# Eight heads as eight 64 x 32 tiles of the TensorE array, in place of block-diagonal pairs

## The chip, the cores and the metric

One core of a Trainium2 chip runs the kernel. The metric is the device time of one execution in microseconds; lower is better. Every time here is of a run on the chip or of its trace.

## What is computed

Eight batches of 576 tokens, eight heads of 64. Each head has 32 packing queries `p` of its own. All products are in fp32, and the answer has the shape [4608, 512].

```python
p_packed = sm_attn(p, k, v)                # 32 packed values for each head, from 576 tokens
out = sm_attn(q, p_packed, p_packed)       # every token attends to the 32 packed values of its head
x = out as [B * S, H * D]                  # 4608 tokens of 512
logits = x @ w_gate; e_idx = argmax(logits)            # 8 experts, one for each token
for e in range(E):
    h = relu(x[mask] @ w1[e])              # 512 -> 1024
    out[mask] = gate_w * eom * (h @ w2[e]) # 1024 -> 512
```

## The kernel before

The work of a batch has three parts, written as Python generators that yield an estimate of their time, and traced in turn so that one batch's attention lies between the matmuls of another's experts. While `ffn(b)` is traced, `route(b + 1)` and `encode(b + 2)` are advanced along with it, up to three quarters of the way (`r1`, `e1`), and at its end `values_up(b + 1)` is merged in. The first batches have their order written out by hand (`CFG["order"]`), with matmuls on zeros (`keep_warm`) where TensorE would wait. Within the traced order a scheduler may put a ready instruction ahead of one that is not.

- `encode(b)` (L254) makes the packed values. The eight heads are two groups g of four, and a group is two pairs c of heads. `p` is copied into `pb`, which holds for each pair 128 rows (two heads of 64 dimensions) and 64 columns (two heads of 32 queries), zero off the diagonal blocks (L257 to L260). `scores` (L234) multiplies it with `k`: one 128-row, 64-column product for a pair, the two pairs beside each other in the columns of the array (`beside`, L79), for half of the tokens (288) at a time, into one PSUM bank. `soft` (L263) is the softmax of a group: the maximum on DVE (L267), the exponential on ACT with its sum (L273). `turn` (L281) transposes it on TensorE, `pack` (L297) multiplies with `v` (`ps_pp`), and L302 scales and masks the result to the two heads' own blocks (`mask`). `expand_T` (L242) transposes both groups; `ppT` is then block-diagonal in the same way as `pb`. `ps_pg` (L329) is the router's product, and `guess` (L337) chooses the expert whose weights the batch loads first: that of evenly weighted packed values.
- `route(b)` (L350): `match` (L363) multiplies `ppT` with `q` (`ps_s2T`), again for each pair; DVE transposes it in blocks of 32, and `soft` (L371) is the softmax over the 32 packed values. `ps_lg` (L401) is the router.
- `values_up(b)` (L504) multiplies `ppT` with the first weights of the guessed expert (`ps_G`), since the attention's weights can be applied after them; `split` (L65) makes of it a high and a low part (`Gh` by ACT, `Gl` by DVE), for products that need one pass. `ffn(b)` (L521) is then `ps_h` (attention's weights with `G`), relu on ACT and DVE, and `ps_o` (second weights).
- Tokens whose expert is not the batch's go through `leftover` (L595) at the end.

PSUM has eight banks, in two tags: `a` with `NA = CFG["pa"] = 3` banks, for the attention, and `f` with the other five, for `ps_h`, `ps_o`, `ps_G` and the scores of the first batches. Loads are issued on SP's queue in the order of the trace; `fetch` (L190) issues one tile of `k`, `q` or `v` where one is given up.

The lines that put products beside each other:

```python
def beside(dsts, seqs):
    for j, row in enumerate(zip(*seqs)):
        for dst, (a, m) in zip(dsts, row):
            res = nc.tensor.matmul(dst, a, m, start=j == 0, stop=j == len(seqs[0]) - 1)
def sides(ps):
    return [ps[c * M2:(c + 1) * M2] for c in range(GP)]      # M2 = 64, GP = 2
```

Of the kernel before, what the change touches and what calls it, by code (L numbers as in the profile page):

```python
# [9 lines left out]
F32 = mybir.dt.float32  # L10
# [10 lines left out]
CFG = dict(pre='kkkkqqkkkk', last=(4, 2, 3), warm=(8, 2, 2, 2, 2, 2), raw=8, a1T=2, rq=2, pa=3, wst=3, w1=6,  # L21
# [10 lines left out]
def tile_packed_attn_then_moe(ctx, tc, qT, kT, v, v_rem, pT, w_go, w1, w2, out):  # L32
    """qT, kT: [B, NG, (2 D), HG / 2, S]; v: [B, NG, 128, TF, (HG D)], its last tokens in v_rem;
    pT: [B, (2 D), H / 2, NP]; w_go: [128, DM / 128, 2 E]; w1, w2: [E, chunk, 128, 2, 512]."""
    nc = tc.nc
    B, NG, _, GP, S = qT.shape
    NPAIR, NP = pT.shape[2:]
# [27 lines left out]
    def split(hi, lo, src, hi_eng=None, lo_eng=None):  # L65
        """src = hi + lo, each of the width that a single-pass product takes."""
        (hi_eng or nc.scalar.copy)(hi, src)  # L67
        (lo_eng or nc.vector).tensor_tensor(lo, src, f(hi), ALU.subtract)  # L68
# [10 lines left out]
    def beside(dsts, seqs):  # L79
        """Products that stand beside each other in the array's columns, in turn."""  # L80
        for j, row in enumerate(zip(*seqs)):
            for dst, (a, m) in zip(dsts, row):
                res = nc.tensor.matmul(dst, a, m, start=j == 0, stop=j == len(seqs[0]) - 1)  # L83
        return res

    def sides(ps):
        return [ps[c * M2:(c + 1) * M2] for c in range(GP)]
# [14 lines left out]
    def keep_warm(b, i):  # L102
        """Work for the tensor engine while the first batch has it wait, for its clock's sake."""
# [13 lines left out]
    odd = const.tile([P, HG], F32, name="odd")  # L117
    nc.gpsimd.memset(odd, 1.0)
    nc.gpsimd.affine_select(out=odd, in_=odd, pattern=[[-NP, HG]], compare_op=ALU.is_ge,
                            fill=0.0, base=0, channel_multiplier=1)  # L120
    nc.gpsimd.affine_select(out=odd, in_=odd, pattern=[[NP, HG]], compare_op=ALU.is_ge,
                            fill=0.0, base=NP - 1, channel_multiplier=-1)
    mask = const.tile([P, 2, 1], F32, name="mask")
    for i in range(2):
        nc.gpsimd.tensor_tensor(mask[:, i], odd[:, i:i + 1], odd[:, i + 2:i + 3], ALU.add)
# [7 lines left out]
    pb = const.tile([P, NPAIR, 2, NP], F32, name="pb")  # L133
    nc.gpsimd.memset(pb, 0.0)
# [34 lines left out]
    pp_d = tc.dram_tile([B, P, NG, P], F32, name="pp_d")  # L169
# [3 lines left out]
    def beyond(gen):  # L173
        """A step of gen, queued behind the anchors."""
# [15 lines left out]
    def fetch(x):  # L190
        """The next of the loads of k, v and p or of q, in the order of their use."""
# [6 lines left out]
        if x == "v":  # L198
            t = sb.tile([P, T, HG * D], F32, tag=tag, name="vt", bufs=bufs)
            nc.sync.dma_start(t[:, 0:TF], v[b, g])  # L200
            nc.sync.dma_start(t[:REM, TF], v_rem[b, g])
        else:
            t = sb.tile([P, GP, S], F32, tag=tag, name=x, bufs=bufs)
            src = (kT if x == "k" else qT)[b, g]
            step = 1 if b == 0 else GP
            for c in range(0, GP, step):
# [35 lines left out]
    def expand_T(b, src, nm):  # L242
        """[(h n), (2h d)] of the groups, zeros but for a row's own head -> [(2h d), group, (h n)]."""
        ps = bank(f"ps_{nm}")
        pv = ps[:, :NG * P].rearrange("p (g n) -> p g n", n=P)
        for g in range(NG):
            t = nc.tensor.transpose(pv[:, g], src[g], ident)  # L247
        anchor(b, t)
        keep_warm(b, 4)
        x = sb.tile([P, NG, P], F32, tag="ppT", name=nm, bufs=CFG["tt"])  # L250
        anchor(b, nc.scalar.copy(x, pv))
        return x

    def encode(b):  # L254
        """p, k, v of a batch -> packed values, transposed and block-diagonal."""
        pt = take("p", b, 0) if ("p", b, 0) in loaded else (fetch("k"), take("p", b, 0))[1]
        for i in range(2):  # L257
            rows = slice(i * D, (i + 1) * D)
            eng(b, "p").tensor_copy(pb[rows, :, i], pt[rows])
        pbs = [pb.rearrange("p c i n -> p c (i n)")[:, c] for c in range(NPAIR)]  # L260
        ppbd = []

        def soft(g, kTs):  # L263
            s1 = [scores(b, pbs[g * GP:(g + 1) * GP], kTs, "s1", "a" if b > 1 else "f", hf) for hf in range(2)]
            nm2 = sb.tile([P, 2], F32, tag="nm2", name="nm2", bufs=2)
            for hf in range(2):
                nc.vector.tensor_reduce(nm2[:, hf:hf + 1], s1[hf], axis=AX.X, op=ALU.max, negate=True)  # L267
            nmx = sb.tile([P, 1], F32, tag="nmx", name="nmx", bufs=2)
            anchor(b, nc.vector.tensor_scalar(nmx, nm2[:, 0:1], nm2[:, 1:2], QK, ALU.min, ALU.mult))
            a1 = sb.tile([P, 2, HS], F32, tag="row", name="a1", bufs=CFG["row"])  # L270
            sm = sb.tile([P, 2], F32, tag="sm", name="sm", bufs=2)
            for hf in range(2):
                anchor(b, nc.scalar.activation(a1[:, hf], s1[hf], AF.Exp, bias=nmx, scale=QK, accum_out=sm[:, hf:hf + 1]))  # L273
            if g == NG - 1:
                keep_warm(b, 1)
            rs = sb.tile([P, 1], F32, tag="rs", name="rs", bufs=2)
            nc.vector.tensor_scalar(rs, sm[:, 0:1], sm[:, 1:2], 1e-9, ALU.add, ALU.add)
            nc.vector.reciprocal(rs, rs)
            return a1, rs

        def turn(g, a1):  # L281
            """The softmax of a group, transposed."""
            a1f = a1.rearrange("p a b -> p (a b)")
            ps = bank("ps_a1T")
            pv = ps.rearrange("p (t n) -> p t n", n=P)
            pr = bank("ps_a1T")
            for t_ in range(TF):
                nc.tensor.transpose(pv[:, t_, :], a1f[:, t_ * P:(t_ + 1) * P], ident)  # L288
            anchor(b, nc.tensor.transpose(pr[:REM, :P], a1f[:, SF:S], ident))
            at = sb.tile([P, T, P], F32, tag="a1T", name="a1T", bufs=CFG["a1T"])  # L290
            copy = nc.vector.tensor_copy if b == 0 else nc.scalar.copy
            anchor(b, copy(at[:, 0:TF], pv))
            anchor(b, copy(at[:REM, TF], pr[:REM, :P]))
# [3 lines left out]
        def pack(g, at, rs, vt):  # L297
            pp = bank("ps_pp")[:, :P]
            anchor(b, beside(sides(pp), [[(at[:n, t_, c * M2:(c + 1) * M2], vt[:n, t_, c * P:(c + 1) * P])
                                          for t_ in range(T) for n in (P if t_ < TF else REM,)] for c in range(GP)]))  # L300
            bd = sb.tile([P, 2, D], F32, tag="bd", name="ppbd", bufs=CFG["bd"])
            anchor(b, nc.vector.scalar_tensor_tensor(bd, pp.rearrange("p (h d) -> p h d", d=D), rs,  # L302
                                                     mask.to_broadcast([P, 2, D]), op0=ALU.mult, op1=ALU.mult))
            bd = bd.rearrange("p h d -> p (h d)")
            ppbd.append(bd)
            nc.sync.dma_start(pp_d[b, :, g], bd)

        xs = []
        for g in range(NG):
            ks = pairs("k", b, g)  # L310
            yield Y["k"]
            xs.append(soft(g, ks))
            yield Y["s1"]
        ats = []
        for g in range(NG):
            ats.append(turn(g, xs[g][0]))
            yield Y["a1T%d" % g]
        for g in range(NG):
            vt = take("v", b, g)
            follow("v", b)  # L320
            pack(g, ats[g], xs[g][1], vt)
            yield Y["pp"]
        x = expand_T(b, ppbd, "ppT")
        ppT = [x[:, c // GP, c % GP * M2:(c % GP + 1) * M2] for c in range(NPAIR)]
        yield Y["ppT"]
        ps_g = bank("ps_pg")
        pg_v = ps_g[:, :NG * 2 * E].rearrange("p (g e) -> p g e", e=2 * E)
        for g in range(NG):
# [538 lines left out]
```

## Time and profile before

| | us |
|---|---|
| median of 3 runs | 481.17 (479.87 to 481.31) |
| span of the profiled execution, first to last instruction | 478.5 |
| TensorE busy (PE), matmuls | 465.0, 97% |
| weight loads (PEld) | 342.0, 71% |
| VectorE (DVE) | 286.5, 60% |
| ScalarE (ACT) | 166.4, 35% |
| GpSimd (POOL) | 101.2, 21% |
| DMA queue of the loads, share of 16 engines | 48.9% |

The profiled execution's own time is its span; 2.67 us lie between it and the median of the runs. PE is TensorE's matmuls, PEld its weight loads, which overlap them. A row of a group gives the line, engine, operation, output<-inputs, the tile of the array that an instruction uses (rows*columns), the shape of what it reads, and behind the bar the busy time in us and the mean ns of one; busy time counts overlapping instructions once. A row of the timeline gives start and length in us and, behind x, how many of the kind it merges. Clock 1.00 is the full TensorE clock.

### The profile page before, as it was taken

The numbers are of one execution on the slowest core, as the hardware profiler recorded it, in microseconds if no ns is written. First come the engines' busy times: TensorE is split into PE (matmuls) and PEld (weight loads), VectorE is DVE, ScalarE is ACT, GpSimd is POOL, SyncE is SP. The second block draws the span as 40 slices with busy tenths as digits, with TensorE's granted clock in tenths as the row PEclk, the third lists the DMA queues.
The fourth block names the chain that finished last, engine by engine and source line by source line (L and its number), as shares of the span: only waits on it lengthen the run. The fifth ranks groups of instructions, "written<-read, shape, count | busy, mean of one in ns | idle before, by whom it ended". The sixth has DMA issues, their size and how long they took to land.

```text
span 478.5 us, 8004 instructions
## 1 busy us (share of the span) xinstructions
PE 465.0 (97%) x2864; PEld 342.0 (71%) x2864; DVE 286.5 (60%) x793; ACT 166.4 (35%) x376; POOL 101.2 (21%) x99
## 2 busy tenths in 40 slices
PE   6999999999999999999999999999999999979996
PEld 4648766878667785878767786777858885765755
DVE  4594784697367645575457644586457846971221
ACT  2174343524224333243225333353333333410310
POOL 6114110621007200341006200160004400410000
PEclk8999999999999999999999999999999999979999
DMA  8899992549506950197404920186102920255101
GB/s 260 287 391 379 372 340 64 176 170 381 171 28 216 400 171 6 53 358 271 134 12 154 367 82 3 33 293 241 50 12 79 344 74 11 68 186 205 41 5 53
DMA packets 39113, 83.05 MB, mean 174 GB/s; under 512 B 3999, under 2 KB 18719, under 8 KB 39072
## 3 DMA queue, kind: packets, MB, share of 16 engines
q1 hardware_dynamic: 39040, 82.52, 48.9%
q8 instruction: 23, 0.38, 0.3%
q14 instruction: 18, 0.15, 0.1%
q0 software_dynamic: 32, 0.00, 0.0%
HBM read 66.78 MB, written 15.79 MB: 173 GB/s over the span
## 4 chain that ended last, share of the span: by engine, by line
PE 92%; DVE 4%; POOL 2%; ACT 1%; issue 1%; POOLq 0%
PE ps_o L573 36%; PE ps_h L76 22%; PE ps_o L585 7%; PE ps_G L83 6%; PE ps_pp L83 5%; PE ps_s2T L83 4%; PE ps_s L83 4%; PE ps_a1T L288 1%; PE ps_lg L83 1%; PE ps_lo L682 1%; PE ps_lh L682 1%; POOL keys L145 1%; ACT a L273 1%; PE ps_pg L83 1%; PE ps_ppT L247 1%
## 5 line engine op out<-in xcount | busy, mean ns | idle before, releaser
L573 PE MATMUL ps_o<-w2h,hT 128*128 128x512 f32 (+1 forms) x528 | 168.7, 393 | 0.0
L573 PEld LDWEIGHTS ps_o<-w2h,hT 128*128 128x128 f32 x528 | 97.5, 189 | 29.2 <-issue 5.1
L573 PE MATMUL ps_o<-w2l,hT 128*128 128x512 f32 (+1 forms) x264 | 103.0, 390 | 0.0
L542 DVE SCALAR_TENSOR_TENSOR hT<-ps_h,hT 128x256 fp32r<-128x256 f32 x192 | 60.9, 350 | 42.9 <-ACT hT L539 42.1
L68 POOL TENSOR_TENSOR w2l<-wst,w2h 128x1024 fp32r<-128x1024 f32 x25 | 66.2, 2651 | 93.5 <-ACT w2h L67 77.8
L76 PE MATMUL ps_h<-ah,Gh 128*128 128x256 f32 (+1 forms) x256 | 80.6, 315 | 3.4 <-DVE l_dec L630 1.9
L539 ACT ACTIVATE hT<-ps_h 128x320 fp32r<-128x320 f32 (+1 forms) x128 | 51.3, 411 | 92.8 <-PE ps_h L76 91.9
L76 PE MATMUL ps_h<-al,Gh 128*128 128x256 f32 (+1 forms) x256 | 77.7, 303 | 0.0
L76 PE MATMUL ps_h<-ah,Gl 128*128 128x256 f32 (+1 forms) x256 | 76.6, 299 | 0.0
L76 PEld LDWEIGHTS ps_h<-ah,Gh 128*128 128x128 f32 x256 | 48.9, 191 | 17.6 <-issue 7.6
L573 PEld LDWEIGHTS ps_o<-w2l,hT 128*128 128x128 f32 x264 | 50.0, 189 | 9.5 <-issue 0.4
L76 PEld LDWEIGHTS ps_h<-al,Gh 128*128 128x128 f32 x256 | 49.0, 192 | 4.0 <-issue 3.3
L76 PEld LDWEIGHTS ps_h<-ah,Gl 128*128 128x128 f32 x256 | 49.0, 191 | 0.1
L67 ACT CAST w2h<-wst 128x1024 fp32r<-128x1024 f32 x32 | 33.6, 1049 | 44.1 <-PE ps_o L573 37.4
L576 DVE TENSOR_SCALAR ob<-ps_o,scm_all 128x512 f32<-128x512 f32 (+1 forms) x33 | 24.0, 727 | 27.7 <-PE ps_o L573 26.7
L68 DVE TENSOR_TENSOR Gl<-ps_G,Gh 128x512 fp32r<-128x512 f32 x32 | 21.9, 684 | 24.5 <-ACT Gh L67 24.4
L83 PE MATMUL ps_G<-w,ppT 128*64 128x512 f32 x128 | 33.2, 613 | 0.0
L67 ACT CAST Gh<-ps_G 128x512 fp32r<-128x512 f32 x32 | 18.8, 587 | 28.3 <-PE ps_G L83 28.2
L432 POOL TENSOR_TENSOR g_d<-L,g_mx 128x40 f32<-128x40 f32 x8 | 2.1, 266 | 124.0 <-DVE g_mx L418 124.0
L384 POOL TENSOR_TENSOR s<-s,sm 128x576 f32<-128x576 f32 x14 | 16.2, 1159 | 52.5 <-DVE sm L383 46.8
L585 PE MATMUL ps_o<-w2h,hT 128*128 128x512 f32 x64 | 27.2, 425 | 0.0
L585 PE MATMUL ps_o<-w2l,hT 128*64 128x512 f32 x64 | 24.1, 394 | 0.0
(170 smaller groups left out, 527.4 us busy)
## 6 DMA issues: line engine op xcount, KB each, us to landing
w<-in_w_dram SPq DMA_DIRECT2D x40, 512.0 KB, 5.7
wst<-in_w_dram SPq DMA_DIRECT2D x32, 512.0 KB, 8.2
vt<-in_v_dram SPq DMA_DIRECT2D x16, 512.0 KB, 5.7
k<-in_kT_dram SPq DMA_DIRECT2D x14, 576.0 KB, 8.3
q<-in_qT_dram SPq DMA_DIRECT2D x14, 576.0 KB, 6.9
out_dram<-ob SPq DMA_DIRECT2D x31, 256.0 KB, 2.2
a_d<-a2T SPq DMA_DIRECT2D x16, 320.0 KB, 4.5
out_dram<-ob SPq DMA_DIRECT2D x10, 128.0 KB, 2.3
```

The source lines that it names most:

```text
L67: (hi_eng or nc.scalar.copy)(hi, src)
L68: (lo_eng or nc.vector).tensor_tensor(lo, src, f(hi), ALU.subtract)
L76: res = nc.tensor.matmul(dst, a, m, start=j == 0, stop=j == len(seq) - 1)
L83: res = nc.tensor.matmul(dst, a, m, start=j == 0, stop=j == len(seqs[0]) - 1)
L145: nc.gpsimd.tensor_scalar(keys.rearrange("p b n -> p (b n)"), key_i, big_id, None, ALU.add)
L384: eng(b, "mul").tensor_tensor(sv, sv, sm.to_broadcast([P, n, NP]), ALU.mult)
L539: nc.scalar.activation(hT[:, :n], ps, AF.Relu)
L542: nc.vector.scalar_tensor_tensor(hT[:, d0:d0 + s1 - s0], ps[:, s0:s1], 0.0, f(hT[:, s0:s1]), op0=ALU.max, op1=ALU.subtract)
L573: nc.tensor.matmul(ps[:, cs], a, m[:, cs], start=i == 0, stop=i == len(seq) - 1)
L576: nc.vector.tensor_scalar_mul(ob[:, cs], ps[:, cs], sc)
L585: nc.tensor.matmul(ps[:n], a, m, start=i == 0, stop=i == len(seq) - 1)
L682: nc.tensor.matmul(ps[i % nq * m:(i % nq + 1) * m], stat[:, i], wt[:, k], start=i < nq, stop=i >= n - nq)
```

## The change

The block-diagonal form goes. A head is now a tile of 64 rows (its dimensions) and 32 columns (its packed values). A group is now the four even or the four odd heads: rows 0 to 63 of a tile hold an even head, rows 64 to 127 the odd one of its pair. `by_head` issues the eight heads' products in turn, a group to a PSUM bank, in column 32c for pair c. `k` and `q` are loaded by halves of the tokens, for all heads, in place of by groups; `encode` scores both halves for both groups before the first softmax. `pack` has products of 32 columns by 64 in place of 64 by 128, both groups in one bank, and no mask. `ppT` is one 128 x 128 transpose in place of two. The last 64 tokens' transposes of both groups share a bank and a copy. `pa` is 4 in place of 3, so tag `f` has four banks. `values_up` takes two banks at a time and yields once for both. `leftover` follows the new layout, with four banks for `xT` in place of two. The host's layout of `q`, `k`, `v`, `w1` follows.

```diff
-CFG = dict(... pa=3, ...)
+CFG = dict(... pa=4, ...)
...
     def sides(ps):
-        return [ps[c * M2:(c + 1) * M2] for c in range(GP)]
+        return [ps[c * NP:(c + 1) * NP] for c in range(NPAIR)]
+
+    def by_head(banks, stat, mov):
+        at = [(g, c) for c in range(NPAIR) for g in range(NG)]
+        return beside([sides(banks[g])[c] for g, c in at],
+                      [[(stat[g * D:(g + 1) * D, c * NP:(c + 1) * NP], mov[c][g * D:(g + 1) * D])] for g, c in at])
...
-    pb = const.tile([P, NPAIR, 2, NP], F32, name="pb")
-    nc.gpsimd.memset(pb, 0.0)
...
-    def scores(b, stat, mov, nm, tag, hf):
-        ps = bank(f"ps_{nm}", tag)[:, :HS]
-        x = beside(sides(ps), [[(stat[c], mov[c][:, hf * HS:(hf + 1) * HS])] for c in range(GP)])
+    def scores(b, stat, mov, nm, tag):
+        ps = [bank(f"ps_{nm}", tag)[:, :HS] for _ in range(NG)]
+        x = by_head(ps, stat, mov)
...
         def turn(g, a1, pr):
...
-            anchor(b, nc.tensor.transpose(pr[:REM, :P], a1f[:, SF:S], ident))
+            anchor(b, nc.tensor.transpose(pr[:REM, g], a1[:, SF:S], ident))
...
+        def pack(pp, g, at, ar, vt):
+            return beside(sides(pp[:, g]), [[(at[:, t_, c * NP:(c + 1) * NP], vt[:, t_, c * D:(c + 1) * D])
+                                             for t_ in range(TF)]
+                                            + [(ar[:REM, g, c * NP:(c + 1) * NP], vt[:REM, TF, c * D:(c + 1) * D])]
+                                            for c in range(NPAIR)])
...
+        s1 = []
+        for hf in range(2):
+            ks = pairs("k", b, hf)
+            yield Y["k"]
+            s1.append(scores(b, pt, ks, "s1", "a" if b > 1 else "f"))
+            for g in range(NG):
+                anchor(b, nc.vector.tensor_reduce(nm2[:, g, hf:hf + 1], s1[hf][g], axis=AX.X, op=ALU.max, negate=True))
+            yield Y["s1"]
+        a1s = [soft(g, s1) for g in range(NG)]
...
+        pr = bank("ps_a1r")[:, :NG * P].rearrange("p (g n) -> p g n", n=P)
         for g in range(NG):
-            ats.append(turn(g, xs[g][0]))
+            ats.append(turn(g, a1s[g], pr))
             yield Y["a1T%d" % g]
+        ar = sb.tile([P, NG, P], F32, tag="a1r", name="a1r", bufs=1)
+        anchor(b, (nc.vector.tensor_copy if b == 0 else nc.scalar.copy)(ar[:REM], pr[:REM]))
+        pp = bank("ps_pp")[:, :NG * D].rearrange("p (g d) -> p g d", d=D)
...
+        anchor(b, nc.vector.tensor_tensor(ppc, pp, rs.to_broadcast([P, NG, D]), ALU.mult))
+        nc.sync.dma_start(pp_d[b], ppc)
...
+        anchor(b, nc.tensor.transpose(ps, ppc, ident))
...
+        ps_g = [bank("ps_pg")[:, :2 * E] for _ in range(NG)]
+        anchor(b, by_head(ps_g, ppT, [wgo[:, c] for c in range(NPAIR)]))
...
         for part in ([0], [1]) if b == 0 else ([0, 1],):
+            for hf in part:
+                match(hf)
+                yield Y["s2T"]
             for g in range(NG):
-                match(g, part)
-                yield Y["s2T"]
                 soft(g, part)
...
         for n in range(DF // BANK):
-            for g in range(NG):
-                ps = bank("ps_G", "f")
-                beside(sides(ps), [[(ppT[g * GP + cc], w1s[(n * NG + g) * GP + cc])] for cc in range(GP)])
+            banks = [bank("ps_G", "f") for _ in range(NG)]
+            by_head(banks, ppT, w1s[n * NPAIR:(n + 1) * NPAIR])
+            for ps in banks:
...
-                yield 0.86
+            yield 0.86
...
-        for cc in range(GP):
-            rows, cs = slice(cc * M2, (cc + 1) * M2), slice(cc, NPAIR, GP)
-            pv = bank("ps_l", "f")[:, :NG * m].rearrange("p (c n) -> p c n", n=m)
-            for g in range(NG):
-                nc.tensor.matmul(pv[:, g], pp[rows, g], at_[rows, g], start=True, stop=True)
-            nc.scalar.copy(xT[:, cs], pv)
+        pv = [bank("ps_l", "f")[:, :m] for _ in range(NPAIR)]
+        for g in range(NG):
+            hd = slice(g * D, (g + 1) * D)
+            beside([x[hd] for x in pv], [[(pp[c * NP:(c + 1) * NP, hd], at_[c * NP:(c + 1) * NP, g])] for c in range(NPAIR)])
+        for c in range(NPAIR):
+            nc.scalar.copy(xT[:, c], pv[c])
```

More of the change, by code (lines that the diff above doesn't have):

```diff
@@ L116, in tile_packed_attn_then_moe @@
     nc.scalar.activation(first, blank[:, 0:1], AF.Exp)
[L117 to L125, printed above, removed]
     ones = const.tile([P, P], F32R, name="ones")
@@ L198, in fetch @@
         if x == "v":
-            t = sb.tile([P, T, HG * D], F32, tag=tag, name="vt", bufs=bufs)
+            t = sb.tile([P, T, NPAIR * D], F32, tag=tag, name="vt", bufs=bufs)
             nc.sync.dma_start(t[:, 0:TF], v[b, g])
@@ L202, in fetch @@
         else:
-            t = sb.tile([P, GP, S], F32, tag=tag, name=x, bufs=bufs)
+            t = sb.tile([P, NPAIR, HS], F32, tag=tag, name=x, bufs=bufs)
             src = (kT if x == "k" else qT)[b, g]
-            step = 1 if b == 0 else GP
-            for c in range(0, GP, step):
+            step = NPAIR // 2 if b == 0 else NPAIR
+            for c in range(0, NPAIR, step):
                 nc.sync.dma_start(t[:, c:c + step], src[:, c:c + step])
@@ L240, in scores @@
         return ps
-    def expand_T(b, src, nm):
-        ps = bank(f"ps_{nm}")
-        pv = ps[:, :NG * P].rearrange("p (g n) -> p g n", n=P)
-        for g in range(NG):
[L247 to L252, printed above, removed]
     def encode(b):
         pt = take("p", b, 0) if ("p", b, 0) in loaded else (fetch("k"), take("p", b, 0))[1]
[L257 to L265, printed above, removed]
-            for hf in range(2):
[L267 to L273, printed above, removed]
@@ L274, in soft, with turn @@
             if g == NG - 1:
                 keep_warm(b, 1)
[L276 to L283, printed above, removed]
+            return a1.rearrange("p a b -> p (a b)")
+        def turn(g, a1, pr):
             ps = bank("ps_a1T")
             pv = ps.rearrange("p (t n) -> p t n", n=P)
-            pr = bank("ps_a1T")
@@ L287, in turn @@
             for t_ in range(TF):
-                nc.tensor.transpose(pv[:, t_, :], a1f[:, t_ * P:(t_ + 1) * P], ident)
-            anchor(b, nc.tensor.transpose(pr[:REM, :P], a1f[:, SF:S], ident))
-            at = sb.tile([P, T, P], F32, tag="a1T", name="a1T", bufs=CFG["a1T"])
+                nc.tensor.transpose(pv[:, t_, :], a1[:, t_ * P:(t_ + 1) * P], ident)
+            anchor(b, nc.tensor.transpose(pr[:REM, g], a1[:, SF:S], ident))
+            at = sb.tile([P, TF, P], F32, tag="a1T", name="a1T", bufs=CFG["a1T"])
@@ L291, in turn @@
             copy = nc.vector.tensor_copy if b == 0 else nc.scalar.copy
-            anchor(b, copy(at[:, 0:TF], pv))
-            anchor(b, copy(at[:REM, TF], pr[:REM, :P]))
+            anchor(b, copy(at, pv))
             keep_warm(b, 2 + g)
             return at
[L297 to L306, printed above, removed]
@@ L320, in encode @@
             follow("v", b)
[L321 to L324, printed above, removed]
+            anchor(b, pack(pp, g, ats[g], ar, vt))
+            if g == 0:
+                yield Y["pp"]
+        ppc = sb.tile([P, NG, D], F32, tag="ppc", name="ppc", bufs=CFG["bd"])
+        anchor(b, nc.vector.tensor_tensor(ppc, pp, rs.to_broadcast([P, NG, D]), ALU.mult))
+        ppc = ppc.rearrange("p g d -> p (g d)")
+        nc.sync.dma_start(pp_d[b], ppc)
+        yield Y["pp"]
+        ps = bank("ps_ppT")[:, :P]
+        anchor(b, nc.tensor.transpose(ps, ppc, ident))
+        keep_warm(b, 4)
+        ppT = sb.tile([P, P], F32, tag="ppT", name="ppT", bufs=CFG["tt"])
+        anchor(b, nc.scalar.copy(ppT, ps))
         yield Y["ppT"]
-        ps_g = bank("ps_pg")
-        pg_v = ps_g[:, :NG * 2 * E].rearrange("p (g e) -> p g e", e=2 * E)
-        for g in range(NG):
-            anchor(b, beside(sides(pg_v[:, g]), [[(ppT[c], wgo[:, c])] for c in range(g * GP, (g + 1) * GP)]))
+        ps_g = [bank("ps_pg")[:, :2 * E] for _ in range(NG)]
+        anchor(b, by_head(ps_g, ppT, [wgo[:, c] for c in range(NPAIR)]))
         keep_warm(b, 5)
         pg = sb.tile([P, NG, 2, 2 * E], F32, tag="pg", name="pg", bufs=CFG["pg"])
-        anchor(b, nc.vector.tensor_copy(pg, pg_v.rearrange("p g (i e) -> p g i e", i=1).to_broadcast([P, NG, 2, 2 * E])))
+        for g in range(NG):
+            anchor(b, nc.vector.tensor_copy(pg[:, g], ps_g[g].rearrange("p (i e) -> p i e", i=1).to_broadcast([P, 2, 2 * E])))
         R[b], packed[b] = (ppT, pg), ppT
@@ L352, in route @@
         qTs = []
-        for g in range(NG):
-            qTs.append(pairs("q", b, g))
+        for hf in range(2):
+            qTs.append(pairs("q", b, hf))
             yield Y["q"]
@@ L359, in route, with match @@
         A[b] = (ah, al)
-        rows = {}
-        def match(g, part):
-            if g not in rows:
-                rows[g] = sb.tile([P, 2, HS], F32, tag="row", name="s2", bufs=CFG["row"])
-            for hf in part:
-                ps = scores(b, ppT[g * GP:(g + 1) * GP], qTs[g], "s2T", "a" if b else "f", hf)
-                nc.vector.transpose(rows[g][:, hf], ps)
+        rows = [sb.tile([P, 2, HS], F32, tag="row", name="s2", bufs=CFG["row"]) for _ in range(NG)]
+        def match(hf):
+            ps = scores(b, ppT, qTs[hf], "s2T", "a" if b else "f")
+            for g in range(NG):
+                nc.vector.transpose(rows[g][:, hf], ps[g])
         def soft(g, part):
```

58 lines of the change are left out of this document (31 added, 27 removed).

## The prediction

> **What bounds the kernel now.** I read the busy shares and the chain first, then the waits of TensorE, then stretches, then the products that the change touches.
>
> ```profile
> span 478.5 us, 8004 instructions
> PE 465.0 (97%) x2864; PEld 342.0 (71%) x2864; DVE 286.5 (60%) x793; ACT 166.4 (35%) x376; POOL 101.2 (21%) x99
> PE 92%; DVE 4%; POOL 2%; ACT 1%; issue 1%; POOLq 0%
> ```
>
> The waits of TensorE (what waited, for what; us in total, times, longest):
>
> ```profile
> PE ps_s L83 <- POOL keys L145: 2.9, 1, 2.9
> PE ps_h L76 <- DVE l_dec L630: 1.9, 1, 1.9
> PE ps_a1T L288 <- ACT a L273: 1.2, 1, 1.2
> ...
> PE ps_h L76 <- DVE ob L576: 1.1, 1, 1.1
> PE ps_h L76 <- DVE hT L542: 0.4, 1, 0.4
> ```
>
> TensorE works or drains in 97% of the span, the chain runs on it for 92%, and each place where it waits for another engine occurs once. So a microsecond taken off TensorE is a microsecond off the end, if nothing else becomes late. By stretches (length, then busy time and count of PE, PEld, DVE, ACT, POOL, then granted clock, DMA share, GB/s):
>
> ```profile
> 5.00:10.00 5.00, 2.21 (x12) 1.49 (x14) 3.10 (x3) 0.00 (x0) 3.62 (x7) 0.82 1.00 347
> 10.00:15.00 5.00, 4.87 (x33) 3.29 (x32) 3.65 (x14) 2.15 (x8) 0.00 (x0) 0.83 1.05 374
> 20.00:25.00 5.00, 3.81 (x32) 2.09 (x31) 4.48 (x17) 1.56 (x5) 1.53 (x3) 1.00 0.50 168
> ...
> 203.10:258.20 55.10, 55.10 (x346) 40.84 (x345) 32.56 (x93) 20.55 (x46) 11.53 (x10) 1.00 0.50 178
> ...
> 368.40:404.00 35.60, 35.60 (x210) 26.36 (x210) 24.08 (x66) 13.18 (x30) 7.28 (x6) 1.00 0.43 156
> 404.00:430.00 26.00, 22.64 (x109) 19.37 (x108) 22.85 (x42) 7.54 (x13) 7.99 (x3) 0.87 0.34 112
> ```
>
> Three regimes: a start in which the DMA engines are full (share near 1) but for about half of 20 to 25 us; a repeating batch of 55.1 us in which PE is busy all the time, DVE at 59% and DMA at 50%; and a tail from 404 us in which DVE (22.85 of 26) plans the leftovers, which the change does not touch. The change is worth what it saves PE up to 404 us.
>
> **How the products run now.** Rows of one batch (start, length, count):
>
> ```profile
> 203.04 1.19 PE L83 MATMUL ps_s2T<-q,ppT 128*64 128x288 f32 x8
> 205.79 0.71 PE L83 MATMUL ps_s<-k,pb 128*64 128x288 f32 x4
> 227.65 2.85 PE L83 MATMUL ps_pp<-vt,a1T 128*64 128x128 f32 x40
> 233.12 0.64 PE L83 MATMUL ps_lg<-a2T,pg 128*32 128x128 f32 x16
> 238.13 1.08 PE L83 MATMUL ps_G<-w,ppT 128*64 128x512 f32 x4
> 239.14 0.44 PE L247 MATMUL ps_ppT<-ident,ppbd 128*128 128x128 f32 x2
> 241.00 1.94 PE L83 MATMUL ps_G<-w,ppT 128*64 128x512 f32 x8
> 250.71 0.41 PE L83 MATMUL ps_pg<-wgo,ppT 128*64 128x16 f32 x8
> 120.28 1.09 PE L83 MATMUL ps_pp<-vt,a1T 128*64 128x128 f32 x16
> ```
>
> The code issues 8 products a batch for ps_G and the trace has 16 matmuls: a product is two matmuls. I call a round one matmul in every tile that runs beside the others. Two tiles are beside each other now, so x8 is four rounds and x4 two: a score round costs (1.19 − 0.71)/2 = 0.24 us and a call's fixed part 0.71 − 0.48 = 0.23; a ps_G round (1.94 − 1.08)/2 = 0.43, fixed 0.22. For ps_pp eight rounds in 1.09, less the same 0.22, is 0.109 a round; its 20 rounds are 2.18 of 2.85, so 0.67 is fixed.
>
> **Do smaller tiles overlap?** All hangs on that; the nearest rows are four 32-column tiles (ps_lg) and two tiles of 64 rows (ps_l, of the leftover):
>
> ```profile
> 42.44:42.50 0.06, 0.05 (x4) 1.00 1.62 614
> 431.86:431.90 0.04, 0.03 (x2) 1.00 1.50 614
> 431.87 0.64 PE L672 MATMUL ps_l<-l_a,l_pp 64*128 64x32 f32 x8
> L83 PE MATMUL ps_lg<-a2T,pg 128*32 128x128 f32 x128 | 5.6, 279 | 0.0
> L76 PE MATMUL ps_lg<-a2T,pg 128*32 128x64 f32 x32 | 3.1, 219 | 0.0
> L672 PE MATMUL ps_l<-l_a,l_pp 64*128 64x32 f32 x8 | 0.6, 278 | 0.0
> ```
>
> The first row is ps_lg alone: four matmuls start within 0.06 us, in four column tiles. Its 16 take 0.64: less 0.28 for one, 0.12 for each of three more rounds of four. The second is ps_l alone: two start within 0.04 us, and the code puts one set of its products in rows 0 to 63, the other in 64 to 127. Its 8 take 0.64: (0.64 − 0.28)/3 = 0.12 a round of two; one after another they would take 0.28 + 7 × 0.12 = 1.12. So four column tiles run together, and so do two row tiles; that four times two do is the step no row shows. I take it, since each direction does alone. Start offsets I charge at another 0.06 a call, from the first row.
>
> **The sum, part by part, for one batch.** Rounds now hold eight tiles (four for ps_pp); fixed parts stay.
> - Scores of k (ps_s): PE now 2.55 (row below). After: two calls of two rounds, 2 × (0.48 + 0.23 + 0.06) = 1.54. Saves 1.01.
> - Scores of q (ps_s2T): 2.60 to 1.54, saves 1.06.
> - ps_G: 4.09 to 2 × (0.86 + 0.22 + 0.06) = 2.28, saves 1.81.
> - ps_pp: 64 moving columns; the ps_lg row of that width gives 3.1/8 = 0.39 for four in turn, so (0.39 − 0.22)/3 = 0.056 a round. 20 rounds, 1.12 + 0.67 + 0.06 = 1.85, against 2.85: saves 1.00. Its last 64 tokens still change from 128 rows to 64, as now.
> - ps_ppT: one transpose less, 0.44 to 0.30 (0.14). ps_pg: four rounds in 0.41 become two; (0.41 − 0.21)/3 = 0.07 each: about 0.1 with the offsets off again. Together 0.2.
>
> Sum 5.08 a batch.
>
> ```profile
> 203.10:258.20 55.10, 2.55 (x16) 1.00 0.50 178
> 203.10:258.20 55.10, 2.60 (x18) 1.00 0.50 178
> 203.10:258.20 55.10, 4.09 (x16) 1.00 0.50 178
> 203.10:258.20 55.10, 2.85 (x40) 1.00 0.50 178
> 36.00:368.40 332.40, 15.61 (x98) 1.00 0.51 179
> ```
>
> These are ps_s, ps_s2T, ps_G and ps_pp alone in one batch, then ps_s2T from 36 to 368 us: 98 matmuls, six batches and a bit, as the others have six. So that stretch gives 6 × 5.08 = 30.5, and the last ps_s2T (14 of 16 matmuls) and ps_G, behind it in the stretch to 404 us, 0.93 + 1.81 = 2.7. Together **33.2**.
>
> A rule bears on the fixed part: the Trainium skill, "TensorEngine Tiling (Array Packing)", section "Key Properties", says that changing the tiling mode drains the array. The trace agrees: the 0.67 of ps_pp holds its three changes of row count. By the row the drains are in the fixed parts that I keep; if by the rule each of the seven calls a batch paid one more, at a third of 0.67, that would be 1.5 us a batch, 10 in all, and the sum below 459.
>
> **The start.** The copies of p into a block-diagonal pb go. One of them was held to the end of the POOL's keys (L145), and PE waited 2.9 us; then the clock stood at 0.82 and 0.83 for 10 us. Only the half-idle DMA of 20 to 25 us can be recovered before the first weights, 2.5 us; behind that PE's saving for encode(1), route(0) and ps_G, 1.01 + 1.00 + 1.06 + 1.81 = 4.9, meets full DMA queues. Best −7.4; worst +1.2, since the softmax of a group now starts only when both halves of the tokens are scored (the ps_a1T wait, once more). I take −4.
>
> **What is added or moved.** Engines other than PE: DVE gets a second copy to pg and loses one ppbd, ACT copies half of ppT, POOL loses pb; DVE's 59% is the cover, and at nothing I cost them; without it the pg copy (0.23, DVE) is in series, 1.6 us over seven batches. SP: pp_d is one DMA a batch in place of two; k and q tiles hold the same bytes a partition (2 × 576 or 4 × 288 floats), so no queue gets longer. PSUM is the price:
>
> ```profile
> 56.86 1.10 PE ps_h L76 x6
> L67 ACT CAST Gh<-ps_G 128x512 fp32r<-128x512 f32 x32 | 18.8, 587 | 28.3 <-PE ps_G L83 28.2
> L68 DVE TENSOR_TENSOR Gl<-ps_G,Gh 128x512 fp32r<-128x512 f32 x32 | 21.9, 684 | 24.5 <-ACT Gh L67 24.4
> ```
>
> ps_h, ps_o and ps_G share four banks instead of five. Where ps_h waited for DVE (three rows above), PE now stops one group of six earlier, 1.10 each: 3.3; between 0 and one a batch, 7.7. ps_G takes its banks in pairs; the second is free after 0.59 (ACT) and twice 0.68 (DVE), 2 us, during which PE has ps_o: nothing in the likeliest case. The scores of k hold all four banks of the other tag until the exponentials; behind them stand the transposes, then ps_pp. The ps_a1T row prices a miss at 1.2: 0 to eight batches, 9.6; I take one, as now there is one. The leftover's four banks for xT in place of two: 0 to 1.1, half. Sum +5, between 0 and 18.4.
>
> **Sum:** 478.5 − 33.2 − 4 + 5 = 446.3 for the profiled span. The runs' median is 481.17; 2.7 us lie around the span. So 449. Ends: 478.5 − 33.2 − 7.4 + 2.7 = 441 and 478.5 − 33.2 + 1.2 + 18.4 + 2.7 = 468.
>
> **Rivals.**
> 1. Columns overlap, rows do not. Then calls keep four rounds: ps_s 2 × (0.96 + 0.23) = 2.38, ps_s2T the same, ps_G 2 × (1.72 + 0.22) = 3.88: 0.17 + 0.22 + 0.21 saved, with ps_pp and the rest 1.8 a batch, 11.9 in all; start −3, banks +5: 471. Against it the x2 row of ps_l.
> 2. The banks cost their upper ends in every batch: 467. For it, pairs from a pool of four; against, that PE now waits on DVE three times in all.
> 3. Slower: the change does not get eight at once. If the two matmuls of a product follow one another in strict order, only the second of one tile and the first of the next overlap: 8 products take 9 rounds. ps_s 2 × (9 × 0.24 + 0.23) = 4.78 (+2.2), ps_s2T likewise (+2.2), ps_G 2 × (9 × 0.43 + 0.22) = 8.2 (+4.1), ps_pp about even: +8.5 a batch, 6.5 batches +55, about 540. It decides as soon as fewer than two tiles run together. Against: by it ps_lg's 16 would be 9 rounds, 0.28 + 8 × 0.12 = 1.24, not 0.64. Such an order is a rule of the Trainium skill, "TensorE: Matmul & The Clock Gate", section "Part 3: Packing small matmuls — row/col tiling": matmuls start and end in program order. By that rule the trace's four starts within 0.06 us need the halves to be interleaved already when issued; no row here shows this for eight tiles.
>
> **How the numbers follow.** A difference under 0.3% (1.4 us) cannot be told from none. The forecast 449 (441 to 468) 0.78; rival 2 0.07, rival 1 0.07; rival 3 0.05; savings and waits that cancel, within 0.3%, 0.03. Faster 0.92, same 0.03, slower 0.05. The range 439 to 468 holds the forecast and rival 2, and 2 us below for fewer, longer calls than now (ps_s comes as x4, x4, x8, three fixed parts; two after).
>
> **What would show it.** Right: eight ps_s matmuls starting within 0.12 us; busy time of ps_s, ps_s2T and ps_G a batch near 1.5, 1.5 and 2.3, ps_pp 1.9; period near 50 us with PE still above 95%; the first ps_s at 5 to 6 us in place of 7.8. Wrong: ps_s near 2.4 (rival 1); idle PE before ps_h, ps_G or ps_a1T with DVE or ACT as the releaser (rival 2); nine score rounds a call (rival 3).

## The result: 459.3 us, ten more than forecast, and the profile after

| | before | after |
|---|---|---|
| median (lowest to highest, runs) | 480.52 us (479.62 to 481.31, 4) | 459.27 us (458.59 to 460.66, 4) |
| ratio, 95% interval | | 0.957 (0.955 to 0.959) |
| span of the profiled execution | 478.5 us | 459.0 us (460.66 with what lies around it) |

Times and ratios go by the fast runs alone, those within 1.5% of a kernel's fastest; of the first experiment three runs of six were slower, the profiled one among them.

The page of the changed kernel, its head and the shares of the chain by engine:

```profile
span 459.0 us, 9479 instructions
PE 433.6 (94%) x3632; PEld 325.2 (71%) x3632; DVE 276.1 (60%) x782; ACT 165.1 (36%) x371; POOL 93.8 (20%) x79
PE 85%; DVE 8%; DMA 3%; issue 1%; SPq 1%; ACT 1%; ACTq 0%
```

31 us of TensorE's busy time went (465.0 to 433.6), but only 19.5 of the span: its share fell from 97% to 94%, and VectorE's share of the chain rose from 4% to 8%. Where it waits (what waited, for what; us, times, longest):

```profile
PE ps_lg L81 <- DVE a2T L367: 10.0, 2, 6.0
PE ps_h L74 <- DVE ob L559: 2.0, 1, 2.0
PE warm L116 <- ACT a L249: 1.7, 1, 1.7
PE ps_h L74 <- DVE hT L525: 1.7, 1, 1.7
```

Between what left TensorE and what left the span are 12 us, by which its idle time rose. The largest new item is 10.0 us in two waits, of 3.9 and 6.0, in which the router of the first batch waits for VectorE. Next the repeating batch (stretch, length, TensorE's busy time and count of one product, granted clock, DMA share, GB/s): `ps_s`, `ps_s2T`, `ps_G` and `ps_pp`, then `ps_s` in the 0.06 us in which one call starts.

```profile
201.70:252.20 50.50, 1.43 (x32) 1.00 0.54 193
201.70:252.20 50.50, 1.43 (x32) 1.00 0.54 193
201.70:252.20 50.50, 3.22 (x32) 1.00 0.54 193
201.70:252.20 50.50, 1.80 (x80) 1.00 0.54 193
204.77:204.83 0.06, 0.05 (x8) 1.00 1.27 410
```

Eight tiles do start together, within 0.05 us, and `ps_s` came down from 2.55 to 1.43 us, `ps_s2T` from 2.60, `ps_pp` from 2.85 to 1.80. `ps_G` did not follow: 4.09 to 3.22. The period fell from 55.1 to 50.5.

Where the start stands is told by the first `ps_h` of a batch. Three rows of the changed kernel (first, third and eighth batch), each one instruction with its duration in ns and, behind it, its start; then the third batch of the kernel before:

```profile
L74 PE MATMUL ps_h<-ah,Gh x1: 562/562/562, 42.9 to 42.9; 128*128 128x256 f32 x1
L74 PE MATMUL ps_h<-ah,Gh x1: 279/279/279, 151.2 to 151.2; 128*128 128x256 f32 x1
L74 PE MATMUL ps_h<-ah,Gh x1: 279/279/279, 400.2 to 400.2; 128*128 128x256 f32 x1
```

```profile
L76 PE MATMUL ps_h<-ah,Gh x1: 280/280/280, 147.1 to 147.1; 128*128 128x256 f32 x1
```

| us | before | after | difference |
|---|---|---|---|
| first `ps_h`, batch 1 | 34.0 | 42.9 | +8.9 |
| first `ps_h`, batch 3 | 147.1 | 151.2 | +4.1 |
| first `ps_h`, batch 8 | 414.9 | 400.2 | −14.7 |
| end of the span | 478.5 | 459.0 | −19.5 |

So up to the third batch the changed kernel is *behind*, with less work done by TensorE. And the first of these took 562 ns, in the kernel before 386. The stretches of the start (columns as in the prediction's stretches), then the first 50 us of the changed kernel and of the one before:

```profile
20.00:25.00 5.00, 2.26 (x32) 0.72 (x32) 5.00 (x17) 1.75 (x4) 2.68 (x4) 0.96 0.73 260
25.00:30.00 5.00, 0.64 (x4) 0.19 (x4) 4.45 (x19) 0.88 (x3) 0.00 (x0) 0.50 1.01 400
30.00:36.00 6.00, 2.15 (x22) 1.18 (x26) 3.15 (x8) 3.23 (x10) 0.00 (x0) 0.50 1.02 409
36.00:42.00 6.00, 6.00 (x37) 1.17 (x29) 5.49 (x20) 4.66 (x11) 3.14 (x3) 0.50 1.03 356
...
0.00:50.00 50.00, 34.32 (x418) 21.51 (x419) 29.46 (x92) 18.71 (x46) 16.35 (x28) 0.76 0.93 329
```

```profile
0.00:50.00 50.00, 44.30 (x332) 32.27 (x333) 32.87 (x104) 19.43 (x51) 17.02 (x38) 0.97 0.93 332
```

TensorE is nearly idle from 23 to 33 us, and the clock is at one half from 24.6 to 45.1. The chain of the changed kernel there (start, us, what) says what it is late for:

```profile
22.47 8.14 DMA wst<-in_w_dram
30.63 1.05 ACT w2h L65
31.71 1.23 DVE w2l L66
32.93 0.40 DVE a2T L367
33.38 0.75 PE ps_lg L81 x9
...
35.59 1.86 PE ps_G L81 x8
```

VectorE's queue has the split of the *second* weights (`w2l`), which waits for their DMA by way of ScalarE's `w2h`, ahead of the last transposes of `a2T`: it stands 2.3 us and then splits for 1.2. TensorE's queue has the router (`ps_lg`), which needs `a2T`, ahead of `ps_G`. Nor had `ps_G` all it needs: the four `f` banks held the second batch's `ps_s`, and the exponentials that free them stood in ScalarE's queue behind `w2h` and the router's copy `lgs` and began at 34.9 us; `ps_G` starts at 35.5. In the kernel before `ps_G` started at 25.9 us, and that split came behind it.

The diff moves none of this openly. But the first batches are traced by a hand-written string of generator steps (`order`), and the change gave the generators fewer stops: `route(0)` seven in place of nine, `values_up` two in place of four. So the same letter of the string now stands for a later piece of work.

### The profile page after: what moved, and what is told of

Its sections match the earlier page's. It is cut to its first block, busy times and chain, and to the rows that moved or that the text cites. A ratio compares the mean times of both kernels' runs of the same rounds, so it can differ in the third digit from the quotient of the medians.

```text
span 459.0 us, 9479 instructions
## 1 busy us (share of the span) xinstructions
PE 433.6 (94%) x3632; PEld 325.2 (71%) x3632; DVE 276.1 (60%) x782; ACT 165.1 (36%) x371; POOL 93.8 (20%) x79
## 4 chain that ended last, share of the span: by engine, by line
PE 85%; DVE 8%; DMA 3%; issue 1%; SPq 1%; ACT 1%; ACTq 0%
PE ps_o L556 36%; PE ps_h L74 22%; PE ps_o L568 7%; PE ps_G L81 6%; PE ps_pp L81 3%; PE ps_a1T L260 2%; PE ps_s L81 2%; DMA wst<-in_w_dram 2%; PE ps_s2T L81 2%; DMA k<-in_kT_dram 1%; PE ps_lg L81 1%; PE warm L116 1%; DVE ob L559 1%; PE ps_lh L665 1%; DVE l_tmp L627 1%
## 5 line engine op out<-in xcount | busy, mean ns | idle before, releaser
L74 PE MATMUL ps_h<-al,Gh 128*128 128x256 f32 (+1 forms) x256 | 76.6, 299 | 0.0
L66 POOL TENSOR_TENSOR w2l<-wst,w2h 128x1024 fp32r<-128x1024 f32 x25 | 63.5, 2546 | 50.0 <-ACT w2h L65 47.8
L81 PE MATMUL ps_G<-w,ppT 64*32 64x512 f32 x256 | 29.4, 657 | 0.0
L66 DVE TENSOR_TENSOR w2l<-wst,w2h 128x1024 fp32r<-128x1024 f32 x7 | 13.6, 1940 | 17.5 <-ACT w2h L65 17.5
```

## The experiments

My theory: two things stand between 459.3 and the forecast, neither in the array: the order of the queues at the start, and `ps_G`'s two banks, which come free one after the other. The rivals are in the expectations. Ratios are to the kernel before, with 95% intervals; all but 4 and 8 edit the changed kernel.

**1. The router's stop back.**

```
             for g in range(NG):
                 soft(g, part)
+                if b == 0 and g == 0:
+                    yield Y["s2T"]
```

> The changed kernel with one line more: the router of the first batch stops once more in the hand-written order, after the softmax of its first group, so that it has nine stops as in the kernel before (the change left it seven). No operation is added or left out. Theory A: the change moved no work at the start, but its shorter generators made the hand-written order run the router ahead of the split of the second weights and of ps_G, and TensorE then stood behind ps_lg (waiting for a DVE that waited for the second weights' DMA) and the clock fell to one half for 20 us. Then the first ps_h, at 42.9 us in the changed kernel, comes back to about 34, the half clock near 25 us is gone, and the time falls by 7 to 12 us, to about 449 (ratio to before 0.935). Rival B: the start is late because the softmax of a group needs both halves of the tokens, and because the DMA engines are full: then the wait only changes its name, the first ps_h stays near 42 us and the time at 458 to 461 (ratio 0.955).

Measured: 459.3 us (454.7 to 460.5), ratio 0.956 (0.949 to 0.963): no gain that can be told. The profiled execution took 462.0 us, so only the places of things are read from it; the third experiment's profile has the first `ps_h` of the first and third batch within 0.8 us of them (33.4 and 151.5).

The first `ps_h` of the first and third batch, and a piece of its chain:

```profile
L74 PE MATMUL ps_h<-ah,Gh x1: 385/385/385, 32.6 to 32.6; 128*128 128x256 f32 x1
L74 PE MATMUL ps_h<-ah,Gh x1: 279/279/279, 151.7 to 151.7; 128*128 128x256 f32 x1
```

```profile
26.05 10.03 DMA wst<-in_w_dram
36.10 1.04 ACT w2h L65
37.15 0.48 ACT Gh L65
```

The first half of theory A held (`ps_h` at 32.6 us, with 10.2 us of half clock between 23 and 45 us in place of 20.5), the second did not: by the third batch nothing of the ten microseconds was left. A DMA of the second weights now holds ScalarE until 36.1 us, with the last `Gh` behind it, and `ps_h` waits 2.1 us for its `Gl`. That is rival B's "the wait only changes its name", though not its late `ps_h`.

**2. `ps_G` paced so that both banks are free.** `fl=0.428` becomes 1.5, and in `values_up`

```
-            yield 0.86
+            yield 2.6
```

> The changed kernel with two numbers of its pacing changed: a call of ps_G counts 2.6 instead of 0.86 in the merge with ps_o, and the first waits for 1.5 instead of 0.428, so that each call finds both of its banks free and its eight products stand together in TensorE's queue (in the changed kernel they stand as four of one bank, four of that call with four of the next, four of the last). No operation is added or left out. Theory A: ps_G fell only from 4.09 to 3.22 us a batch because its two banks come free one after the other; then it falls to about 2.3 a batch here and the period by 0.9, over some six and a half batches 6 us: 453 (ratio 0.943). Rival B: eight ps_G tiles of 512 columns do not run together even when they stand together: ps_G stays near 3.2, time 459. Rival C: they do, but the later splits of G make the first ps_h of a batch wait for Gl: ps_G 2.3, TensorE waits for DVE ahead of ps_h once a batch, and the time is 457 to 465.

In the changed kernel (first fence: start, length, count) the queue has four products of one bank (x8, as a product is two matmuls), then eight (four of the other bank, four of the next call), then the last four (two of their matmuls have rows of their own, just ahead of the x6); four products take as long as eight. In the second fence stand the two calls of the paced kernel, in the third `ps_G` alone in one batch of it (columns as above):

```profile
235.71 1.06 PE L81 MATMUL ps_G<-w,ppT 64*32 64x512 f32 x8
237.37 1.09 PE L81 MATMUL ps_G<-w,ppT 64*32 64x512 f32 x16
239.69 1.03 PE L81 MATMUL ps_G<-w,ppT 64*32 64x512 f32 x6
```

```profile
235.68 1.09 PE L81 MATMUL ps_G<-w,ppT 64*32 64x512 f32 x16
240.31 1.09 PE L81 MATMUL ps_G<-w,ppT 64*32 64x512 f32 x16
```

```profile
201.00:250.60 49.60, 2.18 (x32) 1.00 0.54 197
```

`ps_G` is 2.18 us (forecast 2.28), and a batch lasts 49.6 (its first `ps_h` at 201.0 and 250.6): theory A's mechanism, with its price. The time hardly moved, 457.9 us, ratio 0.955 (0.951 to 0.960). By the traces the eighth batch's first `ps_h` comes 5.6 us earlier (394.6 for 400.2), and the tail takes 2.9 of them back: 61.7 us in place of 58.8, with a wait of `ps_h` for VectorE's `ob` of 2.6 in place of 2.0 and twice the time at half clock (6.8 for 3.4).

**3. Both.**

> Both edits together: the router's extra stop of the first batch and the pacing of ps_G. If the start and the banks of ps_G are the two things that stood between the changed kernel and its forecast, the two gains add: about 459.3 - 10 - 6 = 443 (ratio 0.922). Rival: they meet the same limit (the tail's planning on DVE or the DMA engines) and give no more than the larger of the two, 448 to 450.

454.5 us, 0.947 (0.942 to 0.952): neither 443 nor 449, but 5 us less than the changed kernel. In its trace the stop has not mended the start: the third batch begins at 151.5 us here, at 151.2 to 151.7 in the changed kernel and in the first two. That execution took 458.0 us, though, the longest of six (451.8 to 458.0); where the others gained is not shown.

**4. The bank alone,** in the kernel before: `pa=3` becomes `pa=4`.

> The kernel before, with nothing changed but the split of PSUM's eight banks: four instead of five for ps_h, ps_o and ps_G, four instead of three for the rest. The forecast priced this bank at 3.3 us (0 to 7.7), as waits ahead of ps_h. Theory A: the price is real and the changed kernel pays it: 480.5 + 3.3 = 484 (ratio 1.007), with new waits of TensorE for DVE ahead of ps_h. Rival B: the trace of the changed kernel shows no such waits beyond 2.0 us in all, and the fifth bank was used in few places of the kernel before: within 0.3% of before (ratio 0.997 to 1.003).

480.3 us, 1.002 (0.999 to 1.005). Rival B. The forecast's 3.3 us for fewer `f` banks is not there in the time, as long as no call takes them in pairs; the interval leaves room for 2.3. The waits of `ps_h`, all in the tail:

```profile
PE ps_h L76 <- DVE ob L576: 2.1, 1, 2.1
PE ps_h L76 <- DVE hT L542: 1.7, 1, 1.7
```

Two of the three waits of the kernel before are longer, by 1.0 and 1.3 us, as the forecast had it for each, but the third, of 1.9, is gone: 3.8 in place of 3.4, and in the changed kernel 3.7. By this trace the eighth batch's first `ps_h` comes 4.0 us later than in the kernel before (418.9), 3.0 of them by the second batch's, and the tail takes 2.2 back.

**5. The first batch's splits later.** On top of 1: the order string has `RwFFRwFRFeee` in place of `RwFwFRFRFweee`, the first batch reads two chunks ahead, and its splits are queued behind `hT`:

```
+            with ExitStack() as stack:
+                if b == 0 and j and "hT" in tail:
+                    stack.enter_context(tc.issue_after(tail["hT"]))
...
-            if len(waiting) > CFG["ahead"]:
+            if len(waiting) > (CFG["ahead"] if b else 2):
...
-                if len(G[b]) < 4:
+                if len(G[b]) < (4 if b else 0):
```

> The first experiment's kernel, and in it the splits of the first batch's second weights are traced later, behind the splits of ps_G and a few of hT on ScalarE. No operation is added or left out. With the extra stop alone the first ps_h came at 32.6 us, but ScalarE then stood at 36.1 us for a DMA of the second weights, ahead of the last Gh and of hT, and PE lost what it had gained. Theory A: the start is a matter of what stands ahead of what in the queues of ScalarE and DVE; then ps_h runs on through 36 to 40 us, the second batch's first ps_h comes near 88 in place of 93.5, and the time falls to 452 to 456. Rival B: the stretch up to 50 us is bound by the second weights' DMA itself (it lands at 36 to 38 us whatever stands behind it): ps_o waits in place of ps_h and the time stays at 458 to 461.

452.9 us, 0.945 (0.941 to 0.949). Theory A, the third batch at 144.0 in place of 151.2 us, though the second came at 91.2, not near 88. Its first `ps_h` in the third batch, and what TensorE still waits for at the start:

```profile
L77 PE MATMUL ps_h<-ah,Gh x1: 279/279/279, 144.0 to 144.0; 128*128 128x256 f32 x1
```

```profile
PE ps_s2T L84 <- ACT a L252: 2.6, 1, 2.6
```

The same operations, queued otherwise at the start, are worth 6 us. What is left is the second fence: a call of `ps_s2T` waits for two `f` banks that still hold `ps_s` of the second batch.

**6. The second batch's splits on VectorE:** `b1=('al', 'k0', 'ob', 'sub', 'w0', 'w1', 'w2', 'w3')`.

> The changed kernel with the four splits (w2l) of the second batch's second weights on VectorE in place of GpSimd; nothing else. In the changed kernel VectorE's small instructions of the router near 95 to 102 us (g_den, scale_all, scm_all) last 2.0 to 2.4 us each in place of 0.2 and end together with GpSimd's w2l of 2.4 us, and TensorE stands 1.1 us behind them. Theory A: they wait for GpSimd; with the splits on VectorE (1.23 us each) they last 0.2 to 0.4, TensorE does not stand at 100 us, and the time falls by 1 to 3 us (456 to 458). Rival B: VectorE gets 4.9 us more to do there and is late elsewhere: 459 to 462.

458.4 us, 0.958 (0.954 to 0.963): the mechanism of A, but no gain in time that can be told. In the changed kernel, VectorE and then GpSimd from 95 us; then one row of this experiment:

```profile
95.27 2.37 DVE L434 TENSOR_SCALAR g_den<-g_den 128x5 f32<-128x5 f32 x1 [0.31 <-ACT g_den L431]
97.99 2.00 DVE L437 TENSOR_TENSOR scale_all<-g_den 128x5 f32<-128x5 f32 x1
```

```profile
95.21 7.26 POOL L66 TENSOR_TENSOR w2l<-wst,w2h 128x1024 fp32r<-128x1024 f32 x3 [2.89 <-ACT w2h L65]
```

```profile
L434 DVE TENSOR_SCALAR g_den<-g_den x1: 163/163/163, 94.6 to 94.6; 128x5 f32<-128x5 f32 x1
```

Five elements a partition take 2.37 us beside GpSimd's split and 0.16 without it, and TensorE's wait at 103 us is gone. It was 1.1 us, under what a measurement resolves here.

**7. The fifth, the sixth and the pacing of the second.**

> The later splits of the first batch, VectorE's splits in the second, and the pacing of ps_G of the second experiment, together. If each removes a loss of its own: the steady batch of 49.6 us of the second experiment, and a start that is 4 to 8 us shorter than there: 446 to 452 (ratio to before about 0.935). Rival: the start ends at the same time whatever its order, and the time is that of the second and third experiments, 454 to 458.

450.9 us, 0.941 (0.937 to 0.944): within the range of the first case. It differs from the fifth by less than the intervals.

**8. `ps_pp` alone,** in the kernel before: four tiles of 32 columns with 64 moving columns, and the rest in pairs.

```
-            anchor(b, beside(sides(pp), [[(at[:n, t_, c * M2:(c + 1) * M2], vt[:n, t_, c * P:(c + 1) * P])
+            anchor(b, beside([pp[j * NP:(j + 1) * NP, :D] for j in range(HG)],
+                             [[(at[:n, t_, j * NP:(j + 1) * NP], vt[:n, t_, j * D:(j + 1) * D])
```

> One part of the change alone, in the kernel before: ps_pp as four tiles of 128 rows and 32 columns with 64 moving columns, one for each head, in place of two of 64 columns with 128 moving columns; its copy to the block-diagonal ppbd reads the 64 columns twice. All else stays in pairs of heads. By the sum's row for ps_pp (2.85 to 1.85 us a batch) 1.0 a batch, over the seven and a half batches in which TensorE is the bound 6 to 8 us: 473 (ratio 0.985). Rival: ps_pp lies beside waits in the first batch and in the second and third it is given back to VectorE's and the DMA's waits as in the changed kernel: 476 to 478 (ratio 0.992).

474.5 us, 0.991 (0.988 to 0.994): by the time between the two cases, by the ratio the rival's. The part's own gain in one batch is a little above the forecast's 1.00, 2.85 less 1.73:

```profile
202.00:256.00 54.00, 1.73 (x80) 1.00 0.50 181
```

**9. The seventh, with the second batch's `ps_s` in the other banks.**

```
-            s1.append(scores(b, pt, ks, "s1", "a" if b > 1 else "f"))
+            s1.append(scores(b, pt, ks, "s1", "a" if b else "f"))
```

> The seventh experiment's kernel with the k scores of the second batch in the four banks of the tag a (as from the third batch on) in place of the four of the tag f; nothing else. In the fifth and the seventh TensorE still stands for 2.6 and 2.2 us near 21 to 23.6 us: a second call of ps_s2T waits for its two banks until ScalarE has taken the exponentials out of them, and the clock falls to one half behind it (for 13.65 and 6.83 us). Theory A: at the start the pairs of banks bind, as all of ps_s, ps_s2T and ps_G draw on four banks there; with the scores elsewhere that wait and the half clock go, the first ps_h comes 2 to 4 us earlier (28 to 30) and the time falls by 2 to 5 us, to 446 to 449. Rival B: what stands next in line is the DMA of the first and second weights, which land at the same time: the first ps_h stays at 31 to 33 us, or ps_o waits in its place, and the time stays at 450 to 452.

445.5 us, 0.929 (0.926 to 0.933), the fastest: 14 us less than the changed kernel, with its operations (four splits on another engine). The first `ps_h` of the first and third batch, then its longest wait:

```profile
L77 PE MATMUL ps_h<-ah,Gh x1: 386/386/386, 31.8 to 31.8; 128*128 128x256 f32 x1
L77 PE MATMUL ps_h<-ah,Gh x1: 279/279/279, 137.6 to 137.6; 128*128 128x256 f32 x1
```

```profile
PE ps_G L84 <- DMA w<-in_w_dram: 3.1, 1, 3.1
```

The time is theory A's; the way is half rival B's: the first `ps_h` gained 0.5 us, not 2 to 4, as `ps_G` now waits for the first weights' DMA, and the half clock there stayed (6.8 us). The gain came in the two batches behind it (third batch at 137.6 us, in the seventh 144.8). About half of that 7 us is `ps_G`, which takes 6.43 us between 32 and 138 us (64 matmuls) and took 9.94 in the seventh (68): more of its calls run as eight at once (both of the third batch's). Why the scores' banks do that was not taken apart.

**10 and 11. What was needed.** The stop of 1 and the banks of 9 alone; then the pacing of 2 with them.

> The changed kernel with two lines changed: the router's extra stop of the first experiment, and the k scores of the second batch in the banks of the tag a, as in the ninth. Splits and pacing stay as in the changed kernel. The extra stop alone gave nothing (ratio 0.956). Theory A: the four banks that the pairs of scores and of ps_G share at the start are the main loss there, and the order of the splits mattered only because ps_s2T stood behind them: then this kernel alone gets most of the way, first ps_h near 31 us, third batch near 140 us in place of 151.2, time 449 to 452 (ratio 0.937). Rival B: the banks matter only once the splits are out of the way: 456 to 460 (ratio 0.955).

> The same kernel with the pacing of ps_G of the second experiment as well: three small edits to the changed kernel. Theory: the pacing takes 0.87 us off each steady batch wherever the start ends, five to six batches of it count, so 4 to 6 us less than the tenth experiment: 444 to 448 by its theory A, 450 to 455 by its rival. If it comes to no less than the ninth's 445.5, the moved splits of the first batch and VectorE's splits of the second were not needed.

458.5 us, 0.956 (0.952 to 0.961), and 450.1 us, 0.939 (0.935 to 0.944). Rival B: without the moved splits the stop and the banks bring nothing that can be told. The pacing then brings more than I had said (8 us for 4 to 6; by the traces 5.5 of it come before the third batch), and 9's other edits, together, 4.6 more. How that divides between the first batch's splits and VectorE's was not taken apart.

## Why the prediction was right, and where it was ten microseconds off

- **Eight tiles at once: right.** Rival 1 wanted 2.38 us for `ps_s`, rival 3 4.78, the forecast 1.54; it is 1.43. Of the rule on the order of matmuls (the Trainium skill, "TensorE: Matmul & The Clock Gate", "Part 3: Packing small matmuls — row/col tiling"): the eight that start within 0.05 us are followed by the other eight 0.27 us later, which by that rule means that the halves of the products are interleaved when they start, as the prediction said they would have to be.
- **Prices of a round: right.** Saved in a batch on `ps_s`, `ps_s2T` and `ps_pp`: 1.12, 1.17 and 1.05, for 1.01, 1.06 and 1.00. No call shows a further drain, which would put `ps_s` above the 1.54 of the sum; that the result stands at the 459 which the prediction gave for such drains is chance.
- **`ps_G`: mis-sized,** 0.87 us a batch for 1.81. The round was right (2.18 in experiment 2); the sentence that failed is "ps_G takes its banks in pairs ... nothing in the likeliest case". I looked for a stall in front of the pair; instead the queue took each bank as it came, and rounds ran half empty. Over six batches and a bit this is 6 us.
- **The start: wrong,** and the main error. I took −4, with a worst end of +1.2; the first `ps_h` was 8.9 us late. The wait for `pb` did go (first `ps_s` at 4.5 us, 7.8 before), but its calls then stand for the DMA of `k` three times, 1.4 us, and 1.7 us go to the wait that the worst end had named, for the exponentials of both halves (the row of `warm` in the waits after). Still the first `ps_s2T` comes 1.4 us earlier than before, at 18.7 us; the loss lies behind it. There I costed the operations of the start and their DMAs and took the queues' order as given, though the prediction should have counted the stops that the hand-written string steps over. Up to the third batch, start and two batches should have brought −4 − 2 × 5.08 = −14.2; they brought +4.1, 18.3 off. TensorE idled 11.5 us more in the first 150 us (15.7 for 5.7 up to 50 us, and 1.5 for nothing behind that). The half clock took half of the 11.9 us that it was busy at that speed (0.64, 2.15 and 6.00 in the stretches above and 3.1 behind them), 5.9, for at most 1.8 before (the 0.82 and 0.83 of two stretches of 5 us). Up to three batches of `ps_G` at 0.94 (1.81 less 0.87) are the rest. This division is an estimate. Experiments 5 and 9 show that the loss was order, banks and pacing together: with the same operations the third batch comes at 137.6 us. What each is worth alone was not taken apart.
- **Added costs: taken as +5, not there.** The bank alone is 0 in the time (experiment 4), the second batch's `ps_a1T` wait did not come, and 36 to 400 us has hardly a wait (1.5 us). The pairs of banks cost elsewhere: in `ps_G`'s rounds, and at the start in `ps_s2T`. Rival 2 was right in kind, in other places and for other waits; its 467 does not follow from its terms, as 18.4 in the sum in place of 5 makes 462.
- **The tail** gave 4.8 us that I had not asked for (63.6 us from the eighth batch's first `ps_h` in the kernel before, 58.8 after). A part is the clock: it was at one half for 6.8 us there in the kernel before and for 3.4 in this one, which I had not counted. By the halving above that is 1.7 us; the rest stays open, and some of it may be no more than spread, as the tail of experiment 4, whose operations are those of the kernel before, is 61.4.

Together: from the third batch on the forecast, without its added costs, was 37.2 − 14.2 = 23.0 us, and 19.5 + 4.1 = 23.6 came. That these agree is in part luck: the batches gave 18.8, some 4 short by `ps_G`, and the tail the 4.8 that I had not asked for. Of the 12.7 us by which the span missed, 18.3 were lost up to the third batch, and the 5 of added costs that did not come were most of what went the other way. So the mechanism and most prices of the array were right, and the total stands within the range also because the errors had opposite signs.

## What to carry to other kernels

Where the trace order is written by hand or steered by stops in generators, count the stops before and after: a change that merges two loops reorders every queue without a line that says so, and costing its operations will not show it. A change that makes one product fill several banks at once is worth its full price only if the banks come free together; look at the rounds in the trace, not only at the waits. And when a removed wait brings nothing, look at the queue that now holds the same late transfer before giving the cause up: here the router's stop and the pacing each brought nothing that could be told, together 5 us (experiment 3), and with the banks of the scores 9 (experiment 11).

## What the runs showed of the hardware that I had not expected

- **The clock can fall after short waits, and can take long to come back.** In the tenth experiment TensorE stood for 1.8 us, from 94.5; in the fifth for 2.6, from 19.9. Stretches of both (length, TensorE's busy time, granted clock, DMA share, GB/s):

```profile
94.50:96.30 1.80, 0.06 (x2) 1.00 0.03 14
96.30:98.40 2.10, 2.10 (x30) 1.00 0.00 0
98.40:105.20 6.80, 6.80 (x46) 0.50 0.78 281
105.30:109.00 3.70, 3.70 (x24) 1.00 1.02 417
```

```profile
23.00:26.00 3.00, 3.00 (x25) 0.50 0.96 343
...
33.00:36.60 3.60, 3.60 (x26) 0.50 1.03 371
36.70:40.00 3.30, 3.30 (x75) 1.00 1.03 347
```

  A wait of 1.8 us was followed by 6.8 at half clock, an estimated loss of 3.4, and in the second case TensorE was busy all the time for 13.6 us before it got its clock back. Not every such wait does it: in the eleventh experiment one of 1.7 us from 92.3, and in the eighth one of 2.9 from 4.9 and one of 1.7 from 91.0, left the clock at 1.00. The Trainium skill, "TensorE: Matmul & The Clock Gate", section "Why this matters for your kernels", asks for no gaps of more than about 3 us, and for some 4 us of continuous work to reach the full clock; here shorter gaps were enough, and 13.6 us of work were needed.
- **VectorE can stand behind GpSimd,** 2.4 us for an instruction of 0.16 (experiment 6). The Trainium skill, "SBUF — State Buffer", section "SBUF: two separate sides", has this as an exclusive lock on a port pair of the two; the rows agree with it: VectorE's three long instructions (`scm_all` is the third) end at 97.6, 100.0 and 102.5 us, and so do GpSimd's three splits.
